# Second MLP: in-projection as seven block products over 768 tokens, weights summed and split ahead and streamed from DRAM

## The chip, the cores and the metric

One core of one Trainium2 chip runs the whole program in one launch. The metric is device time in microseconds (us), the median over runs of the same kernel. The engines are TensorE (PE, with its weight loads listed apart as PEld), VectorE (DVE), ScalarE (ACT), GpSimd (POOL) and SyncE (SP), whose queue issues all DMAs of this kernel. Every engine takes its own instructions in program order and waits for others at semaphores.

## The reference

2304 tokens of width 512 come out of a small chunked attention, and go through two MLPs one after the other, all in float32:

```python
x = attn_out.transpose(0, 2, 1, 3).reshape(2304, 512)   # attention in chunks of 64 tokens
h = x @ w_in1                                           # 512 -> 2048
x = (h * sigmoid(1.702 * h)) @ w_out1                   # 2048 -> 512
h = x @ w_in2                                           # 512 -> 2048
out = (h * tanh(softplus(h))) @ w_out2                  # 2048 -> 512
```

The weights arrive as 64-bit floats and are turned into float32 on the chip.

## The kernel before

**Three products for one.** Each float32 operand is split into a high part (rounded to the fp32r format) and a low part (the rest), and a product is made of three fp32r matmuls, high by high, high by low, low by high. `mm3` issues them (lines 352 to 354). Each matmul has its own load of 128 stationary columns.

**Tiling.** The tokens are cut into 6 blocks of 384 (`NB`, `TB`), the hidden width of 2048 into 16 slices of 128 (`KF`), the model width of 512 into 4 slices (`KD`). The main loop runs n over 6 x 16 slices of the first MLP, then 6 x 16 of the second. One step n is: `in_proj` for block n // 16 and slice n % 16 (12 matmuls of 128x384 into one PSUM bank of the two with tag `h`), the activation on ACT (`gelu`, or `mish` in the second MLP, line 421), its high part (`g_hi`, line 374) and its low part (`g_lo`, line 378), and, two steps late (`LAG`), the out-projection of slice n - 2: `out_a` in the first MLP (12 matmuls of 128x384 into four banks), `out_b` in the second (9 matmuls of 128x512 into three banks, lines 441 to 443, tokens as stationary operand). After the 16th slice `evac_a` (lines 403 and 404) or `evac_b` (449, 451) empties the banks.

**First MLP, beside it.** While the first block runs, the raw weights of the first MLP are loaded, rescaled (`scale`, line 142, ACT), put together from two integer halves (`join`, lines 152 and 153, DVE) and split (line 174 ACT, 185 DVE); all 32 weight tiles then stay in SBUF (pool `wres`, one tag for each). Blocks 2 to 5 have the attention of the next block between their steps: transposes, scores, softmax, product with v, each a step apart, through one PSUM tag `at`. In the same steps the 32 weight tiles of the second MLP are loaded, joined and stored to DRAM as whole float32 (`w_f`, line 157). In the last block, as the first MLP's tiles fall free, they are fetched (`ws`, line 165) and split, on ACT and POOL, into the same 32 places. The second MLP so has all its weights in SBUF.

**Between the MLPs.** `evac_a` writes the first MLP's result as high and low part over the block's own input. The last two blocks stay in SBUF, the others go to DRAM (`xd`) and are loaded again one block ahead (`load_x2`).

**What sets the order.** The order on every engine is that of the program text (`manual_schedule`). All DMAs go through SP's one queue: each entry waits for its own semaphores, and what stands behind it waits too.

Of the kernel before, what the change touches and what calls it, by code (L numbers as in the profile page):

```python
# [35 lines left out]
def tile_kernel(  # L36
# [32 lines left out]
    xp = ctx.enter_context(tc.tile_pool(name="xp", bufs=2))  # L69
# [7 lines left out]
    class Weights:  # L77
# [8 lines left out]
        def __init__(self, w_in, w_out, staged):  # L86
# [7 lines left out]
            self.first, self.ahead = 0, NRAW - 2 if staged else NRAW  # L94
            self.spare = [] if staged else [f"w{kind}{f}" for kind, f in self.order]
            self.at = {"load": 0, "scale": 0, "join": 0, "fetch": 0, "split": 0}
            self.staged = dram.tile([self.np, P, DM], F32, name="w_f32") if staged else None
# [6 lines left out]
        def load(self):  # L104
            if (i := self._next("load")) is None:
                return
            kind, f = self.order[i]
            r = self.room(f"raw{i}")
            if kind == "i":
                src = self.w_in[:, 2 * f * P : 2 * (f + 1) * P]  # L110
                nc.sync.dma_start(
                    out=r.rearrange("p (k f) w -> p k (f w)", k=KD),
                    in_=src.rearrange("(k p) f -> p k f", p=P),
                )
            else:
                nc.sync.dma_start(
                    out=r.rearrange("p f w -> p (f w)"),
                    in_=self.w_out[f * P : (f + 1) * P, :],
                )
            self.raw[i] = r  # L120
# [7 lines left out]
        def load_ahead(self):  # L128

            used = self.at["join"] if self.staged is not None else self.at["split"] - len(self.open)  # L130
# [7 lines left out]
        def scale(self):  # L138
            if (i := self._next("scale")) is None:
                return  # L140
            hi = self.raw[i][:, :, 1].bitcast(F32)
            nc.scalar.activation(hi, hi, AF.Prelu, scale=2.0**-112, alpha=2.0**32)

        def join(self):
            if (i := self._next("join")) is None:
                return
            r = self.raw.pop(i)
            lo, hi = r[:, :, 0], r[:, :, 1]
            to = hi
            if self.staged is not None:  # L150
                to = half_slot(f"wf{i}").bitcast(I32)
            nc.vector.tensor_scalar(lo, lo, 29, None, op0=ALU.logical_shift_right)
            nc.vector.scalar_tensor_tensor(  # L153
                to, hi, 3, lo, op0=ALU.logical_shift_left, op1=ALU.bitwise_or
            )
            if self.staged is not None:
                nc.sync.dma_start(out=self.staged[i], in_=to.bitcast(F32))
            else:
                self.f32[i] = to.bitcast(F32)

        def fetch(self):
            if (i := self._next("fetch")) is None:
                return
            self.f32[i] = half_slot(f"ws{i}")
            nc.sync.dma_start(out=self.f32[i], in_=self.staged[i])

        def split(self):
# [9 lines left out]
            if self.staged is not None:  # L177
                self.rest()

        def rest(self):  # L180

            eng = nc.vector if self.staged is None else nc.gpsimd
            while self.open:
                key, w, hi, lo = self.open.pop(0)
                eng.tensor_tensor(out=lo, in0=w, in1=hi.bitcast(F32), op=ALU.subtract)  # L185
# [7 lines left out]
        def convert(self):  # L193

            if self.at["join"] > self.at["split"] and self.staged is None:
# [6 lines left out]
            if self.staged is not None or self.at["load"] > 4:  # L202
                self.load_ahead()

# [24 lines left out]
    class Attention:  # L229
# [106 lines left out]
        def x_hi(self, copy):  # L336
            j = self.j
            if j not in xh:
                xh[j] = xp.tile([P, KD, TB], F32R, tag="xh", name=f"xh{j}")
                xl[j] = xp.tile([P, KD, TB], F32R, tag="xl", name=f"xl{j}")  # L340
# [54 lines left out]
    xd, x2 = {}, {}  # L395
# [271 lines left out]
```

## Time and profile before

| what | value |
|---|---|
| time, median of 3 runs | 885.21 us (884.06 to 886.15) |
| profiled execution, first to last instruction | 883.0 us |
| PE busy | 867.3 us, 98% of the span |
| DVE, ACT, POOL busy | 353.2, 277.9, 41.4 us |
| matmuls recorded | 5724 |
| moved by DMA | 82.68 MB, mean 94 GB/s |

The page gives no time of the profiled execution other than its span, so sums below are made against 883.0 us, which is 2.2 us under the median. PE is busy nearly throughout. Matmuls overlap in the pipeline: one is listed with some 335 ns, but the next starts 173 ns later, so the cost of one is read from the distance of starts, not from its duration.

### The profile page before, as it was taken

The page shows a single profiled execution, that of the slowest core. Times are in us where ns is not written, and L with a number is a line of the kernel's source. Part 1 is how long each engine was busy: PE and PEld are TensorE (multiplying, and loading weights), DVE is VectorE, ACT ScalarE, POOL GpSimd, SP SyncE. Part 2 cuts the span into 40 slices and gives each one's busy share as a digit, 9 for nine tenths or more (in the row PEclk, how much of TensorE's full clock was granted, in tenths as well). Part 3 has the DMA queues.
Part 4 walks back from the last instruction along what each step waited for, and adds up shares of the span by engine and source line. Part 5 has one row for each costly group of instructions (what it writes and reads, how often), then busy time and mean ns, then how long its engine had stood idle before and what let it go on. Part 6 is the DMA issues. An engine that isn't in the chain of part 4 may idle for free.

```text
span 883.0 us, 13566 instructions
## 1 busy us (share of the span) xinstructions
PE 867.3 (98%) x5724; PEld 810.6 (92%) x5724; DVE 353.2 (40%) x687; ACT 277.9 (31%) x469; POOL 41.4 (5%) x38
## 2 busy tenths in 40 slices
PE   6999999999999999999999999999999999999998
PEld 4799999999999999999999999999999999999997
DVE  6799554554545555554333222222222222222221
ACT  3898543443324434333434111111111111111111
POOL 0000000000000000001664000000000000000000
PEclk9899999999999999999999999999999999999999
DMA  9968633465438256423442001200200200200100
GB/s 238 269 192 253 170 117 99 108 192 131 108 112 210 76 141 179 115 83 129 128 120 61 1 1 36 72 1 26 83 0 15 94 1 2 107 1 0 37 1 36
DMA packets 91934, 82.68 MB, mean 94 GB/s; under 512 B 58848, under 2 KB 75232, under 8 KB 91872
## 3 DMA queue, kind: packets, MB, share of 16 engines
q1 hardware_dynamic: 91872, 81.80, 31.8%
q8 instruction: 45, 0.74, 0.4%
q14 instruction: 17, 0.14, 0.1%
HBM read 62.39 MB, written 19.40 MB: 93 GB/s over the span
## 4 chain that ended last, share of the span: by engine, by line
PE 91%; DVE 6%; ACT 2%; DMA 1%; issue 0%; DVEq 0%; ACTq 0%
PE h L352 15%; PE h L354 14%; PE h L353 14%; PE acc L354 7%; PE acc L353 7%; PE acc L352 7%; PE accb L443 5%; PE accb L442 5%; PE accb L441 5%; PE third L442 3%; PE third L443 3%; PE third L441 2%; DVE raw L153 1%; PE tr L256 1%; PE pv L328 1%; PE sc L273 1%
## 5 line engine op out<-in xcount | busy, mean ns | idle before, releaser
L374 DVE CAST gh<-t 128x384 fp32r<-128x384 f32 x176 | 69.2, 393 | 437.1 <-ACT t L421 295.8
L352 PE MATMUL h<-xh,wi 128*128 128x384 f32 x512 | 177.3, 346 | 0.0
L354 PE MATMUL h<-xh,wi 128*128 128x384 f32 x512 | 171.6, 335 | 1.2 <-DVE wi L185 1.2
L353 PE MATMUL h<-xl,wi 128*128 128x384 f32 x512 | 171.5, 335 | 0.9 <-DVE xl L348 0.9
L421 ACT ACTIVATE t<-h 128x384 f32<-128x384 f32 x96 | 47.2, 492 | 335.2 <-PE h L354 334.4
L353 PE MATMUL acc<-gl,wo 128*128 128x384 f32 x384 | 128.5, 335 | 1.4 <-DVE gl L378 1.4
L354 PE MATMUL acc<-gh,wo 128*128 128x384 f32 x384 | 128.6, 335 | 0.0
L352 PE MATMUL acc<-gh,wo 128*128 128x384 f32 x384 | 128.3, 334 | 0.0
L378 DVE TENSOR_TENSOR gl<-t,gh 128x384 fp32r<-128x384 f32 x192 | 107.2, 558 | 14.8 <-ACT gh L374 2.7
L352 PEld LDWEIGHTS h<-xh,wi 128*128 128x128 f32 x512 | 96.2, 188 | 3.3
L353 PEld LDWEIGHTS h<-xl,wi 128*128 128x128 f32 x512 | 96.3, 188 | 2.4 <-DVE xl L348 1.2
L354 PEld LDWEIGHTS h<-xh,wi 128*128 128x128 f32 x512 | 96.1, 188 | 1.5 <-DVE wi L185 1.5
L354 PE MATMUL h<-x2h,wi 128*128 128x384 f32 x256 | 86.4, 337 | 0.0
L352 PE MATMUL h<-x2h,wi 128*128 128x384 f32 x256 | 86.2, 337 | 0.0
L353 PE MATMUL h<-x2l,wi 128*128 128x384 f32 x256 | 86.0, 336 | 0.0
L370 ACT ACTIVATE t<-h 128x384 f32<-128x384 f32 x96 | 47.1, 490 | 112.4 <-PE h L354 95.5
L443 PE MATMUL accb<-wo,gl 128*128 128x512 f32 x192 | 76.2, 397 | 0.0
L442 PE MATMUL accb<-wo,gh 128*128 128x512 f32 x192 | 75.8, 395 | 0.0
L441 PE MATMUL accb<-wo,gh 128*128 128x512 f32 x192 | 74.6, 389 | 0.0
L353 PEld LDWEIGHTS acc<-gl,wo 128*128 128x128 f32 x384 | 72.1, 188 | 2.0 <-DVE gl L378 2.0
L354 PEld LDWEIGHTS acc<-gh,wo 128*128 128x128 f32 x384 | 72.1, 188 | 0.0
L352 PEld LDWEIGHTS acc<-gh,wo 128*128 128x128 f32 x384 | 72.1, 188 | 0.0
(83 smaller groups left out, 966.5 us busy)
## 6 DMA issues: line engine op xcount, KB each, us to landing
raw<-in_moe_w_in_dram SPq DMA_DIRECT2D x32, 512.0 KB, 4.5
raw<-in_moe_w_out_dram SPq DMA_DIRECT2D x32, 512.0 KB, 4.5
w_f<-wf SPq DMA_DIRECT2D x32, 256.0 KB, 2.2
ws<-w_f SPq DMA_DIRECT2D x32, 256.0 KB, 2.7
out_dram<-o SPq DMA_DIRECT2D x18, 256.0 KB, 2.1
v<-in_v_dram SPq DMA_DIRECT2D x16, 256.0 KB, 5.8
q<-in_q_dram SPq DMA_DIRECT2D x13, 256.0 KB, 4.9
k<-in_k_dram SPq DMA_DIRECT2D x13, 256.0 KB, 5.4
```

What stands on the lines that cost most here:

```text
L153: nc.vector.scalar_tensor_tensor(to, hi, 3, lo, op0=ALU.logical_shift_left, op1=ALU.bitwise_or)
L256: nc.tensor.transpose(self.pt[:, bank, s], src[:, s], ident)
L352: nc.tensor.matmul(o, wh, mh, start=start, stop=False)
L353: nc.tensor.matmul(o, wh, ml, start=False, stop=False)
L354: nc.tensor.matmul(o, wl, mh, start=False, stop=stop)
L370: nc.scalar.activation(gt[n], hp.pop(n), AF.Gelu_apprx_sigmoid)
L374: (nc.scalar.copy if n < KF else nc.vector.tensor_copy)(gh[n], gt[n])
L378: nc.vector.tensor_tensor(out=gl[n], in0=gt.pop(n), in1=gh[n].bitcast(F32), op=ALU.subtract)
L421: nc.scalar.activation(gt[n], h, AF.Mish)
L441: nc.tensor.matmul(o, a[:, ts], wh, start=f == 0, stop=False)
L442: nc.tensor.matmul(o, a[:, ts], wl, start=False, stop=False)
L443: nc.tensor.matmul(o, b[:, ts], wh, start=False, stop=f == KF - 1)
```

## The change

**What it computes differently.** The second MLP's in-projection is taken for pairs of 384-token blocks and pairs of hidden slices (g and g + 8) as a 2 by 2 block product with seven block products in place of eight: the tokens give 2 x 2 blocks (two token blocks by two halves of the model width), the weights 2 x 2 (two halves of the model width by two slices). Sums and differences of weight blocks (t1 to t4) and of token blocks (s1 to s4) are the operands of products p1 to p7; each product has two k-slices, so 6 matmuls of 128x384. The four results are added up in PSUM (p2 onto p1, p3 onto p5, p4 onto p7) and on DVE (`combine`, line 913).

**What moves.** Weights of the second MLP no longer stay in SBUF. `Second.step` loads, rescales and joins them during steps 16 to 82 of the first MLP, forms the sums on DVE, splits everything into high and low part (ACT and DVE, lines 449, 450, 468, 469) and stores it to DRAM: for each of 8 groups 3.5 tiles of 128x1024 for the in-projection (`w_sums`) and 2 for the out-projection (`w_outs`). In the second MLP these are streamed into 21 places in SBUF (`flow_in`, line 750) once for each of the 3 pairs, each place being refilled as its tile is used up. The result of the first MLP goes to DRAM whole (`x2d`). The token operands p1 to p7 of a pair (`Tokens`, and `Staged` for pairs 1 and 2) are computed beside the work of the pair before, stored to DRAM (`x_ops`, line 725) and loaded into nine homes (`load_home`, line 711), the last five during the pair's last group. POOL's subtraction goes.

```diff
-    def mish(n, h):
-        gt[n] = tmp.tile([P, TB], F32, tag="t", name=f"t{n}")
-        nc.scalar.activation(gt[n], h, AF.Mish)
-        g_hi(n)
-        g_lo(n)
...
     def evac_a(j):
-        for m in range(KD // 2):
-            i = acc[j][m][:, :, 0:TB]
-            ho = xh[j][:, 2 * m : 2 * m + 2, :]
-            lo = xl[j][:, 2 * m : 2 * m + 2, :]
-            nc.scalar.copy(ho, i)
-            nc.vector.tensor_tensor(out=lo, in0=i, in1=ho.bitcast(F32), op=ALU.subtract)
...
+        t = xp.tile([P, KD, TB], F32, tag=f"xh{j % 2}", name=f"x2_{j}")
+        for m, copy in enumerate((nc.scalar.copy, nc.vector.tensor_copy)):
+            copy(t[:, 2 * m : 2 * m + 2, :], acc[j][m][:, :, 0:TB])
+        x2[j] = dram.tile([P, KD, TB], F32, name=f"x2d{j}")
+        nc.sync.dma_start(out=x2[j], in_=t)
...
+        def split(self, w, to, name):
+            n = w.shape[-1] // (2 * P)
+            w = w.rearrange("p (u x) -> p u x", u=n)
+            t = wraw.tile([P, n, 2, 2 * P], F32R, tag="raw", name=name)
+            nc.scalar.copy(t[:, :, 0], w)
+            nc.vector.tensor_tensor(
+                out=t[:, :, 1], in0=w, in1=t[:, :, 0].bitcast(F32), op=ALU.subtract
+            )
+            nc.sync.dma_start(out=to, in_=t.bitcast(F32))
...
+        def step(self, s):
...
+            if k == 0:
+                self.scale(b)
+                self.join(a)
+            elif k == 1:
+                self.load(c)
+                self.join(b)
+                self.sum_b(g, "t1")
+            elif k == 2:
+                self.load(d)
+                for t in ("t2", "t3", "t4"):
+                    self.sum_b(g, t)
+                self.split_sums(g, 0)
+            elif k == 3:
+                self.split_sums(g, 1)
+            elif k == 4:
+                self.scale(c)
+                self.split_sums(g, 2)
+                if nxt:
+                    self.load(("i", g + 1))
+            elif k == 5:
+                self.split_sums(g, 3)
+                self.join(c)
+            elif k == 6:
+                self.scale(d)
+                self.split_out(2 * g)
+                if nxt:
+                    self.load(("i", g + 1 + KF // 2))
+            else:
+                self.join(d)
+                if nxt:
+                    self.scale(("i", g + 1))
...
+        def load_home(q):
+            p, i = divmod(q, len(ORDER))
+            both = put_home(p, ORDER[i])
+            for part, t in enumerate(both):
+                nc.sync.dma_start(out=t.bitcast(F32), in_=ops[p][i, :, part])
...
+        def flow_in(tag):
...
+            t = wres.tile([P, 2, DM], F32R, tag=tag, name="f" + "_".join(map(str, key)))
...
+            nc.sync.dma_start(out=t.bitcast(F32), in_=src)
...
+        for n, (p, g) in enumerate(groups):
+            A, Bk = hb[n % 2], hb[(n + 1) % 2]
...
+            if p + 1 < PAIRS and g == 1:
+                tok = Staged(p + 1, work_room, work_room, None)
+                tok.load()
...
+            go("p1", A)
+            nc.scalar.copy(s1, A)
+            before[0]()
+            go("p6", Bk, stop=True)
+            combine(u2, s1, Bk)
+            spare()
+            before[1]()
+            go("p2", A, start=False, stop=True)
+            gone("s", p, g, 0)
+            low11 = activate(A, s1, f"{n}a")
+            go("p5", Bk)
+            gone("s", p, g, 1)
+            combine(c22, u2, Bk)
+            g11 = low11()
+            spare()
+            before[2]()
+            go("p7", A)
+            combine(c22, c22, A)
+            spare()
+            low22 = activate(c22, c22, f"{n}b")
+            go("p3", Bk, start=False, stop=True)
...
+            combine(c12, u2, Bk)
+            g22 = low22()
+            low12 = activate(c12, c12, f"{n}c")
+            spare()
+            before[3]()
+            go("p4", A, start=False, stop=True)
+            gone("s", p, g, 2)
+            combine(c21, u2, A)
+            g12 = low12()
+            g21 = activate(c21, c21, f"{n}d")()
```

`before[0]` to `before[3]` are the four out-projections of the group before (9 matmuls of 128x512 each), `spare` takes one piece of the next pair's token operands, `gone` refills a place of the stream, and `go` also calls `load_home` in a pair's last group.

On PE in the second MLP a whole in-projection of 12 matmuls stood behind each out-projection. Before (h is the in-projection's bank, accb and third those of the out-projection, x2h and x2l the tokens, wi and wo weights, gh and gl the activations):

```order
L441 MATMUL third_5180<-wo10_4962,gh138_6326 128x512
L442 MATMUL third_5180<-wo10_4962,gh138_6326 128x512
L443 MATMUL third_5180<-wo10_4962,gl138_6328 128x512
L352 MATMUL h13_6395<-x2h0_5620,wi13_5008 128x384
L353 MATMUL h13_6395<-x2l0_5621,wi13_5008 128x384
L354 MATMUL h13_6395<-x2h0_5620,wi13_5008 128x384
```

Now (h_0 and h_1 are the two banks of the products, x0p2 the operand of product p2 of pair 0, fs a streamed tile of weight sums, fo of the out-projection, sum_at, sum_acc0 and sum_acc1 the out-projection's banks):

```order
L875 MATMUL sum_acc1_5301<-fo_0_11_5348,gh3b_5636 128x512
L876 MATMUL sum_acc1_5301<-fo_0_11_5348,gh3b_5636 128x512
L877 MATMUL sum_acc1_5301<-fo_0_11_5348,gl3b_5647 128x512
L848 MATMUL h_0_5173<-x0p2__4879,fs_0_4_0_5140 128x384 x6
L848 MATMUL h_1_5174<-x0p5__4802,fs_0_4_1_5227 128x384 x6
L875 MATMUL sum_at_5299<-fo_0_11_5348,gh3c_5650 128x512
L876 MATMUL sum_at_5299<-fo_0_11_5348,gh3c_5650 128x512
L877 MATMUL sum_at_5299<-fo_0_11_5348,gl3c_5675 128x512
```

Products of 6 matmuls stand singly or in twos between out-projections, and a group of four slices has 42 in-projection matmuls where it had 48.

On SP in the second MLP, between two token blocks, before (o are tiles of the result, x2h and x2l the parts of a token block that is loaded ahead):

```order
L453 DMA out_0_dram<-o4_0_5611 128x512
L453 DMA out_0_dram<-o4_1_5614 128x512
L453 DMA out_0_dram<-o4_2_5617 128x512
L415 DMA x2h0_5620<-xd0_1398 128x1536
L416 DMA x2l0_5621<-xd0_1398 128x1536
```

Now, in the last group of pair 0 (x1p2 and so on are homes of pair 1's operands, each loaded in two halves):

```order
L711 DMA x1p2__6055<-x_ops1_606 128x768 x2
L711 DMA x1p5__6074<-x_ops1_606 128x768 x2
L711 DMA x1p7__6093<-x_ops1_606 128x768 x2
L750 DMA fo_1_1_6096<-w_outs_77 128x1024
L711 DMA x1p3__6107<-x_ops1_606 128x768 x2
L750 DMA fo_1_9_6110<-w_outs_77 128x1024
L750 DMA fs_1_3_0_6124<-w_sums_76 128x1024
L711 DMA x1p4_0_6132<-x_ops1_606 128x768
L711 DMA x1p4_1_6133<-x_ops1_606 128x768
```

SP's queue held five entries for a block's 66 us; now it holds weight tiles all through the second MLP, and the next pair's operands among them.

On DVE in the second MLP nothing but `g_hi` and `g_lo` stood between two blocks. Now, in group 1 of pair 1 (u9, v9 and c9 are the group's partial results, gl the low parts of its activations, a11 to a22 the token blocks of pair 2, s3, s2p1 and s2p5 operands made of them):

```order
L913 TENSOR_TENSOR u9_6316<-u9_6316,h_0_5173 128x384
L545 TENSOR_TENSOR s3_2_6350<-a11_2_6319,a21_2_6323 128x768
L913 TENSOR_TENSOR v9_6317<-u9_6316,h_0_5173 128x384
L864 TENSOR_TENSOR gl9a_6384<-u9_6316,gh9a_6373 128x384
L721 TENSOR_TENSOR s2p1_1_6353<-a11_2_6319,s2p1_0_6352 128x768
L913 TENSOR_TENSOR v9_6317<-v9_6317,h_1_5174 128x384
L545 TENSOR_TENSOR a21_2_6323<-a21_2_6323,a22_2_6325 128x768
L913 TENSOR_TENSOR v9_6317<-u9_6316,h_0_5173 128x384
L864 TENSOR_TENSOR gl9b_6423<-v9_6317,gh9b_6412 128x384
```

The subtraction of a21, which has to arrive by DMA first, stands ahead of the additions that empty the product banks.

## Rows read from the trace of the kernel before

**Rows 1.** Busy time by stage: stretch, length, engines' busy us, granted clock, DMA share, GB/s.

```profile
core 0: us, PE busy (x) PEld busy (x) DVE busy (x) ACT busy (x) POOL busy (x), PEclk, DMA share, GB/s
0.00:28.00 28.00, 20.48 (x271) 13.84 (x272) 16.76 (x33) 12.95 (x22) 0.70 (x6) 0.88 0.92 214
28.00:95.00 67.00, 62.49 (x501) 59.25 (x500) 60.43 (x115) 58.73 (x100) 0.00 (x0) 1.00 0.84 251
95.00:410.00 315.00, 315.00 (x2552) 306.14 (x2551) 159.77 (x309) 121.79 (x188) 0.00 (x0) 1.00 0.45 127
410.00:480.00 70.00, 70.00 (x405) 70.00 (x405) 22.87 (x35) 28.75 (x51) 39.43 (x31) 1.00 0.42 121
480.00:879.40 399.40, 399.35 (x2003) 361.38 (x2001) 93.38 (x198) 55.09 (x110) 1.29 (x1) 1.00 0.07 26
879.40:883.00 3.60, 0.00 (x0) 0.00 (x0) 0.00 (x0) 0.57 (x1) 0.00 (x0) 1.00 0.58 219
```

**Rows 2.** Timeline of PE, one step of the second MLP: start us, duration, instruction.

```profile
481.59 0.33 PE L352 MATMUL h<-xh,wi 128*128 128x384 f32 x1
...
483.50 0.33 PE L354 MATMUL h<-xh,wi 128*128 128x384 f32 x1
483.67 0.39 PE L441 MATMUL accb<-wo,gh 128*128 128x512 f32 x1
...
485.75 0.33 PE L352 MATMUL h<-xh,wi 128*128 128x384 f32 x1
```

**Rows 3.** Groups by line and shape: count | busy us, mean ns | idle before.

```profile
L378 DVE TENSOR_TENSOR gl<-t,gh 128x384 fp32r<-128x384 f32 x192 | 107.2, 558 | 14.8 <-ACT gh L374 2.7 <-DVE gh L374 0.5
L421 ACT ACTIVATE t<-h 128x384 f32<-128x384 f32 x96 | 47.2, 492 | 335.2 <-PE h L354 334.4 <-ACT wo L174 0.8
L404 DVE TENSOR_TENSOR xl<-acc,xh 128x768 fp32r<-128x768 f32 x12 | 11.5, 958 | 2.6 <-ACT xh L403 2.1
L185 DVE TENSOR_TENSOR wo<-raw,wo 128x512 fp32r<-128x512 f32 x16 | 11.0, 686 | 1.0 <-ACT wo L174 0.8
L174 ACT CAST wi<-ws 128x512 fp32r<-128x512 f32 x16 | 9.9, 617 | 2.1 <-DMA ws<-w_f 2.1
L403 ACT CAST xh<-acc 128x768 fp32r<-128x768 f32 x12 | 9.6, 802 | 4.5 <-PE acc L354 4.5
L374 ACT CAST gh<-t 128x384 fp32r<-128x384 f32 x16 | 8.2, 514 | 0.4
```

**Rows 4.** DMA issues: count, KB each, median us from issue to landing.

```profile
raw<-in_moe_w_out_dram SPq DMA_DIRECT2D x32, 512.0 KB, 4.5
...
out_dram<-o SPq DMA_DIRECT2D x18, 256.0 KB, 2.1
...
x2h<-xd SPq DMA_DIRECT2D x4, 768.0 KB, 5.0
x2l<-xd SPq DMA_DIRECT2D x4, 768.0 KB, 6.4
```

**Rows 5.** Busy time by stretch while a token block is loaded, columns as in rows 1.

```profile
552.00:554.00 2.00, 2.00 (x12) 1.82 (x11) 0.38 (x1) 0.00 (x0) 0.00 (x0) 1.00 1.04 347
554.00:556.00 2.00, 2.00 (x12) 1.78 (x11) 0.36 (x1) 0.49 (x1) 0.00 (x0) 1.00 0.96 366
```

**Rows 6.** Timeline of PE in those stretches, first and next matmul row of a change of bank.

```profile
552.74 0.33 PE L352 MATMUL h<-xh,wi 128*128 128x384 f32 x1
...
554.84 0.39 PE L441 MATMUL accb<-wo,gh 128*128 128x512 f32 x1
```

**Rows 7.** Timeline of PE at the start, matmuls at both clock levels.

```profile
1.12 5.30 PE L496 MATMUL idle<-zeros 128*128 128x384 bf16 x16 [1.12 <-DVE zeros L476]
...
13.16 2.94 PE L496 MATMUL idle<-zeros 128*128 128x384 bf16 x17
```

More of the change, by code (lines that the diff above doesn't have):

```diff
@@ L93, in __init__ @@
             self.open = []
[L94 to L97, printed above, removed]
+            self.first, self.ahead = 0, NRAW
+            self.spare = [f"w{kind}{f}" for kind, f in self.order]
+            self.at = {"load": 0, "scale": 0, "join": 0, "split": 0}
         def _next(self, what):
@@ L128, in load_ahead @@
         def load_ahead(self):
[L130 removed]
+            used = self.at["split"] - len(self.open)
             while self.at["load"] < self.np and (
@@ L146, in join @@
                 return
[L147 to L165, printed above, removed]
+            self.f32[i] = join_raw(self.raw.pop(i))
         def split(self):
@@ L551, in tile_kernel @@
+        for n in range(4, NA):
             f = n % KF
@@ new lines, in tile_kernel, with bank @@
+            if n > NA - KF + 3 and n - (NA - KF + 4) < 7:
+                tok.part(n - (NA - KF + 4))
+            if n >= NA - KF:
+                gone = 2 * (f + 1) - min(LAG, f + 1)
+                while flow and gone - 6 > 21 - len(flow):
+                    flow_in(flow.pop(0))
+        hb = [ps.tile([P, TB], F32, tag="h", name=f"h_{i}") for i in range(2)]
+        banks = []
+        shared = {}
+        def bank(i):
+            if not banks:
+                for tag in ("at", "acc0", "acc1"):
+                    t = ps.tile([P, 2, 512], F32, tag=tag, name=f"sum_{tag}", bufs=1)
+                    banks.extend((t[:, 0], t[:, 1]))
+            return banks[i]
@@ new lines, in tile_kernel, with evac_b, last_a @@
+        seen = {(p, h): 0 for p in range(PAIRS) for h in range(2)}
+        def evac_b(p, half):
+            for t in range(TT):
+                i = half * TT + t
+                o = wres.tile([P, DM], F32, tag=work[i % len(work)], name=f"o{p}_{i}")
+                (nc.scalar.copy if i % 2 == 0 else nc.vector.tensor_copy)(o, bank(i))
+                r0 = (2 * p * TT + i) * P
+                nc.sync.dma_start(out=out[r0 : r0 + P, :], in_=o)
+        def last_a(m):
+            out_a(m, m // KF, m % KF)
+            if m == NA - 1:
+                evac_a(m // KF)
@@ new lines, in tile_kernel, with gone, work_room, combine @@
+        before = [lambda: last_a(NA - 2), lambda: last_a(NA - 1), lambda: None, lambda: None]
+        side = []
+        assert not flow
+        def gone(*key):
+            flow_in(place.pop(key))
+        def work_room(name):
+            shared["n"] = shared.get("n", -1) + 1
+            return wres.tile([P, 2, TB], F32, tag=work[shared["n"] % len(work)], name=name)
+        add, sub = ALU.add, ALU.subtract
+        def combine(out, x, h, op=add):
+            nc.vector.tensor_tensor(out=out, in0=x, in1=h, op=op)
@@ L639 @@
+        for i in (0, 2, 1, 3):
+            before[i]()
 _INS = ["q", "k", "v", "moe_w_in", "moe_w_out", "moe2_w_in", "moe2_w_out"]
```

402 lines of the change are left out of this document (290 added, 112 removed).

## The prediction

> **What bounds the kernel now.** I read the busy time by stage first [rows 1]. From 95 us to the last matmul at 879.4 us PE is busy all the time (315.00 of 315.00, 70.00 of 70.00, 399.35 of 399.40 us), at a granted clock of 1.00, the upper of the two levels. In the second MLP DVE works 93.4 and ACT 55.1 of 399.4 us, and the DMA engines are busy for 0.07 of it. So there the time is the number of PE's instructions by their distance, and nothing else ends last. Before 95 us DVE and ACT (60.4 and 58.7 of 67 us) and the loads bound the kernel; the change leaves that part as it is. Next I read the distance of PE's starts in one step of the second MLP [rows 2]: 12 in-projection matmuls take 481.59 to 483.67, 2.08 us or 0.173 us each, and 9 out-projection matmuls 483.67 to 485.75, 2.08 us or 0.231 us each. A matmul's listed duration of 0.33 us covers two neighbours at once and prices nothing. A change of bank is free: from the last in-projection matmul (483.50) to the next bank's first (483.67) are 0.17 us.
>
> **The change, part by part.**
>
> *In-projection of the second MLP.* Removed: 96 steps by 12, 1152 matmuls of 128x384. Added: 24 groups by 7 products by 6, 1008 of the same shape. The difference is 144 by 0.1733 = 25.0 us. All of it lies on PE, which has no idle time there [rows 1], so all of it can be had. The out-projection keeps 24 by 36 = 864 matmuls, and the first MLP its own. A group becomes 42 by 0.1733 + 36 by 0.231 = 7.3 + 8.3 = 15.6 us, the second MLP 24 by 15.6 = 374 us.
>
> *New waits inside a group.* Products use two banks by turns, and each needs DVE or ACT to have read its bank. In a steady group one out-projection (2.08 us) and one product (1.04 us) lie between, 3.1 us of cover. Behind it stand, at most, one addition of 128x384 on DVE (nearest row 0.56 us) or one Mish on ACT (0.49 us) [rows 3]. In order of DVE's queue: five additions and four low parts by 0.56 are 5.0 us a group; beside them in groups 1 to 4 of pairs 0 and 1 some two pieces of token operands, four operations of 128x768 by 0.96, 3.8 us; in all 8.8 of 15.6. ACT has four Mish, four high parts by 0.51 and a copy, 4.5 us, and two casts of 0.80. The narrowest place is the last addition (c21), which stands behind two low parts and a side piece: I find it done 1.7 us before PE wants its bank. The very first group has no out-projections for its last five products, so a cover of 1.04 us against 0.5 to 0.6 us of work and the hand-over. Bounds: 0 and 1 us a pair, 3 in all; I take 0.5, since all but one place have cover of two or more times the work.
>
> *The stream.* A group eats 5.5 tiles of 0.524 MB, 2.88 MB in 15.6 us, 185 GB/s. 21 tiles are asked for ahead of the second MLP; the other 111 (58 MB), the operands of pairs 1 and 2 (3.1 MB read, 11.0 stored, 11.0 loaded), 4.7 MB of results and 0.8 MB of the first MLP's last block make 89 MB in 374 us, 238 GB/s. While a token block was loaded in the kernel before, with PE at full pace, 347 and 366 GB/s went at a share near 1 [rows 5], and the matmuls kept 12 in 2.10 us [rows 6]. So I expect a share of 0.65 to 0.7, and PE unharmed. A tile is asked for some four groups (60 us) before use, against 4.5 us to land [rows 4]. The narrow part is the operands. In a pair's last group 2.88 + 5 by 0.786 = 6.8 MB are asked for in 15.6 us, 436 GB/s: at 350 that ends 3.9 us late. Each home is filled behind the product that frees it and wanted one group later, 18.7 us on; less some 9 us (queue and landing) a margin of 10 us stays. In group 1 DVE waits for the third of four token loads: about 7 us into the group, in pair 1 about 8 us, since the place it lands in holds a result until that is stored; its addition is wanted by PE at 11.4 us. Cost 0 in the forecast. The lower bound of the rate is that of the stages with small pieces, 251 GB/s at a share of 0.84 or 127 at 0.45 [rows 1], both over 280 at full share; then the last group's queue is 9 us, still inside the margin.
>
> What the rows show of many pieces at once is that the two loads of 768 KB, asked for half a microsecond apart, land in 5.0 and 6.4 us [rows 4], so they share the time. The Trainium skill, DMA: Bandwidth & Descriptors (section Bandwidth, Measured), speaks against this change: it asks to batch transfers to 1 MiB and more, and gives 6.15 us for 1 MB alone. By half of that a tile takes an estimated 3.1 us and a group 17 us of transfer, if no two overlap, so the second MLP would be bound by the stream; the trace does not agree, since pieces overlap.
>
> *First MLP.* DVE gains 32 sums of 128x256 (I take 0.43 us, carried down from 0.56 and 0.69 [rows 3]), 40 subtractions of 128x512 by 0.69 and 8 of half that, and the first pair's operands: 14 + 27 + 3 + 10 = 54 us, less 6 of the lighter evacuation. It goes from about half of 315 us to 0.65. ACT gains 40 casts by 0.62 and 8 of half that, 27 us, and loses the 32 casts it did after 410 us. POOL's 39 us go, which nobody waited for. Loads stay, and stores grow from 8.4 to 23 MB. What hides all this is the step of some 4.2 us: what DVE and ACT make in one is used by PE one step later (attention) or two (activations), and PE has not idled with DVE at half load. SP's queue is new at one point: stores wait for DVE, a load waits for the store whose place it takes, and the attention tiles' loads stand behind; those are fetched five steps (over 20 us) ahead. If the cover goes, a transpose or score waits a microsecond or two at some of the 15 attention tiles. Bounds 0 and 8 us; I take 0.5, the nearer row being PE's 315.00 of 315.00.
>
> *The end.* From the last matmul 3.6 us remain [rows 1]: copy, store, landing, as before.
>
> **Sum.** 883.0 - 25.0 + 0.5 + 0.5 = 859.0 us of span; with the 2.2 us by which the median stands above it, **861 us**. PE alone gives 860.2.
>
> **The rivals.**
>
> *Late operands and a busier first MLP.* The 25.0 us are had, but waits at the two pair switches (3 us each if the mixed traffic goes at 235 GB/s in place of 350) and at some attention tiles (up to 8 us) return 3 to 13: 864 to 873, middle 867. For it: SP's queue is in order, and DVE's share grows by a third. Against: margins of 10 us and of a step.
>
> *Hand-offs.* A group has 11 changes between products and out-projections, with two banks that ACT and DVE must clear; before, there were two in 4.2 us with a whole step of cover. If each of 168 products paid 0.1 us, 17 us would go: 878; at 0.15 us nothing is left, 885. Against: changes of bank cost nothing [rows 2, 6]. In the first microseconds, where the granted clock averages 0.88 [rows 1], a matmul of 384 columns took 0.33 us, and 0.173 later [rows 7]: the levels of 1.2 and 2.4 GHz. A tenth of the second MLP at the lower one would cost 37 us and end at 898. The Trainium skill, TensorE: Matmul & The Clock Gate (A second HAM failure mode), tells of a kernel whose clock oscillated because PE idled briefly as it cycled through PSUM banks; the rows here show a clock of 1.00 over 192 such changes.
>
> *The stream bounds the second MLP (slower).* The place is `flow_in` with `x_ops` on one queue. 89 MB in 374 + 25 us is the point from which it decides: below 223 GB/s sustained the kernel is slower than before. At 200 the second MLP takes 445 us and the program 932; at 214, the rate of the first 28 us [rows 1], 416 and 903. For it: the mean demand of 238 lies above that row, reads and writes are mixed, and nothing before ran so for long. Against: that row holds many small attention loads at a share of 0.92, and rows 5 show 347 and more. If pieces did not overlap at all, a group would take 5.5 by the 4.5 us of one tile [rows 4], 24.8 us, 9.2 too many in some 20 groups, and the program 1045; by rows 4 this has hardly a chance, 0.01 of this case.
>
> **How the numbers follow.** Forecast with small waits, 858.5 to 864: 0.74. Late operands or first MLP, 864 to 873: 0.12. Hand-offs with most of the gain lost, 873 to 883.4: 0.05. Within 0.2%, about what a measurement of this kernel can tell from no change: 0.02. Slower, stream or clock: 0.06. Below 858.5: 0.01, as no other PE work goes. The range of 8 in 10 is 858.5 to 869; it leaves out the end of the second case and the rarer ones. Faster 0.92, same 0.02, slower 0.06.
>
> **What would show it.** Right: 5580 matmuls recorded; PE busy all of the second MLP in about 374 us; groups 15.6 us apart; a DMA share near 0.7 there; no PE wait of over a microsecond on an operand or a tile. Wrong: PE waiting for a DMA at the first groups of pairs 1 and 2 or at `fs` and `fo` tiles (stream), for DVE's additions inside groups (hand-offs), for attention tiles after 95 us (first MLP), a granted clock under 1.00, or a distance of matmuls above 0.173 and 0.231 us while the DMAs run.

## The result and the profile after

The changed kernel takes **862.88 us** (median of 4 runs, 861.68 to 863.58) beside 884.97 us of the kernel before on the same chip: a ratio of 0.975, with a 95% interval of 0.9736 to 0.9764. The forecast was 861.0, with a range of 858.5 to 869.0. The profiled execution took 861.68 us, of which 859.9 are its span.

The busy time by stage, to be laid beside [rows 1] (same columns; the second MLP's first product starts at 471.95 us):

```profile
28.00:95.00 67.00, 63.33 (x505) 60.34 (x506) 61.05 (x116) 59.94 (x103) 0.00 (x0) 1.00 0.83 250
95.00:410.00 315.00, 315.00 (x2551) 306.16 (x2550) 192.82 (x380) 141.84 (x229) 0.00 (x0) 1.00 0.53 160
410.00:480.00 70.00, 70.00 (x406) 70.00 (x405) 27.74 (x48) 17.20 (x29) 0.00 (x0) 1.00 0.63 207
480.00:856.00 376.00, 373.53 (x1851) 335.23 (x1849) 138.71 (x245) 122.15 (x237) 0.00 (x0) 1.00 0.68 235
```

The first MLP is read first. DVE went from 159.77 to 192.82 of 315 us and ACT from 121.79 to 141.84, and PE still has 315.00 of 315.00. In the second MLP the DMA engines went from a share of 0.07 to 0.68 at 235 GB/s, with the clock at 1.00 and PE working all but 2.5 of 376 us (0.6 of those lie behind the last matmul). PE's waits from 95 us to the end are three (what waited, for what; us in all, times, longest):

```profile
PE h L848 <- DVE v L913: 0.9, 1, 0.9
PE sum_acc L875 <- ACT o L890: 0.7, 1, 0.7
PE h L848 <- ACT u L858: 0.4, 1, 0.4
```

None is for a tile of the stream. One product and one out-projection of a steady group, to be laid beside [rows 2] (timeline of PE: start, duration, instruction):

```profile
514.75 1.20 PE L848 MATMUL h<-x0p__4763,fs 128*128 128x384 f32 x6
515.79 0.39 PE L875 MATMUL sum_at<-fo,gh2a 128*128 128x512 f32 x1
...
517.64 0.39 PE L877 MATMUL sum_acc<-fo,gl2a 128*128 128x512 f32 x1
517.87 1.23 PE L848 MATMUL h<-x0p__4841,fs 128*128 128x384 f32 x6
518.94 0.39 PE L875 MATMUL sum_acc<-fo,gh2b 128*128 128x512 f32 x1
```

The six matmuls of a product take 1.04 us (514.75 to 515.79), or 1.07 where an out-projection of 512 columns stands ahead of it (517.87 to 518.94), and the nine of an out-projection 2.08 us (515.79 to 517.87), as before. Groups are counted from 0 through all three pairs, and an out-projection is named by the group whose activations it uses; it runs one group later. The starts of one out-projection from group to group lie 15.68 us apart in pairs 0 and 1 and 15.73 in pair 2, up to the last group, with one exception: from group 8 to group 9 it is 17.42 us.

Four stages can now be put beside each other. "Start" ends where the transposes of the attention behind the first token block begin (`at<-ident,e`), the second MLP goes from its first matmul's start to its last one's, and the end is the rest of the span. All are us of the profiled execution; the span is given to 0.1 us, so the ends and their difference are good to about that:

| kernel | start | first MLP | second MLP | end | span |
|---|---|---|---|---|---|
| before | 94.87 | 378.40 | 405.69 | 4.04 | 883.0 |
| after | 93.55 | 378.40 | 383.08 | 4.87 | 859.9 |
| difference | -1.32 | 0.00 | -22.61 | +0.83 | -23.1 |

The -1.32 are no gain of the change: among ten executions of the changed kernel and its variants the start ends between 93.55 and 96.35 us, and this one is the shortest. So the change removed about 21.8 us, where the forecast has 25.0 for the 144 matmuls alone. The experiments ask where the rest went, and whether the covers on which the forecast rested are as thick as it said.

### The profile page after: what moved, and what is told of

Same layout as the page of the kernel before. It is cut to its first block, busy times and chain, and to the rows that moved or that the text cites. A ratio compares the mean times of both kernels' runs of the same rounds, so it can differ in the third digit from the quotient of the medians.

```text
span 859.9 us, 13861 instructions
## 1 busy us (share of the span) xinstructions
PE 841.3 (98%) x5580; PEld 784.9 (91%) x5580; DVE 438.5 (51%) x821; ACT 354.5 (41%) x617; POOL 0.7 (0%) x6
## 4 chain that ended last, share of the span: by engine, by line
PE 87%; DVE 5%; DMA 3%; ACT 3%; issue 0%; SPq 0%; DVEq 0%; ACTq 0%
PE h L848 20%; PE h L342 7%; PE acc L344 7%; PE acc L343 7%; PE acc L342 7%; PE h L343 7%; PE h L344 7%; PE sum_acc L876 5%; PE sum_acc L877 5%; PE sum_acc L875 5%; PE sum_at L877 2%; PE sum_at L876 2%; PE sum_at L875 2%; PE tr L246 1%; DVE raw L190 1%; DMA out_dram<-o 1%
## 5 line engine op out<-in xcount | busy, mean ns | idle before, releaser
L342 PE MATMUL h<-xh,wi 128*128 128x384 f32 x384 | 134.2, 350 | 0.0
L344 PE MATMUL h<-xh,wi 128*128 128x384 f32 x384 | 128.4, 334 | 1.3 <-DVE wi L152 1.3
L343 PE MATMUL h<-xl,wi 128*128 128x384 f32 x384 | 128.5, 335 | 0.9 <-DVE xl L338 0.9
L360 ACT ACTIVATE t<-h 128x384 f32<-128x384 f32 x96 | 47.1, 491 | 129.0 <-PE h L344 119.5
L364 DVE CAST gh<-t 128x384 fp32r<-128x384 f32 x80 | 28.8, 360 | 100.1 <-ACT t L360 100.1
L342 PEld LDWEIGHTS h<-xh,wi 128*128 128x128 f32 x384 | 72.1, 188 | 2.0
L344 PEld LDWEIGHTS h<-xh,wi 128*128 128x128 f32 x384 | 72.1, 188 | 1.6 <-DVE wi L152 1.6
L343 PEld LDWEIGHTS h<-xl,wi 128*128 128x128 f32 x384 | 72.2, 188 | 1.1 <-DVE xl L338 1.1
L913 DVE TENSOR_TENSOR v<-u,h 128x384 f32<-128x384 f32 x48 | 26.6, 553 | 83.8 <-PE h L848 83.8
L368 DVE TENSOR_TENSOR gl<-t,gh 128x384 fp32r<-128x384 f32 x96 | 53.5, 557 | 5.4 <-ACT gh L364 2.7
L858 ACT ACTIVATE v<-v 128x384 f32<-128x384 f32 x48 | 25.2, 525 | 65.6 <-DVE v L913 65.6
L913 DVE TENSOR_TENSOR u<-u,h 128x384 f32<-128x384 f32 x24 | 13.3, 554 | 46.2 <-PE h L848 46.2
L913 DVE TENSOR_TENSOR v<-v,h 128x384 f32<-128x384 f32 x24 | 13.3, 554 | 36.3 <-PE h L848 36.3
L913 DVE TENSOR_TENSOR c<-u,h 128x384 f32<-128x384 f32 x24 | 13.2, 552 | 31.0 <-PE h L848 31.0
```

Source lines behind the costliest of these rows:

```text
L342: nc.tensor.matmul(o, wh, mh, start=start, stop=False)
L343: nc.tensor.matmul(o, wh, ml, start=False, stop=False)
L344: nc.tensor.matmul(o, wl, mh, start=False, stop=stop)
L360: nc.scalar.activation(gt[n], hp.pop(n), AF.Gelu_apprx_sigmoid)
L364: (nc.scalar.copy if n < KF else nc.vector.tensor_copy)(gh[n], gt[n])
L368: nc.vector.tensor_tensor(out=gl[n], in0=gt.pop(n), in1=gh[n].bitcast(F32), op=ALU.subtract)
```

## Experiments

**The kernel again, with two places mended apart and together.** `after_again` is the changed kernel once more. The others stand on it.

> The changed kernel once more, for its time beside the runs that follow: 861.5 to 863.6 us, as in its four runs. In its trace the second MLP from its first in-projection matmul to its last matmul is some 383 us long, the first MLP after 95 us as long as before.

It took 864.48 us (ratio 0.977, 0.9755 to 0.9785), span 862.8. The stages are 96.11, 378.39, 383.44 and 4.86: of the 2.9 us of span by which it differs from the first execution 2.6 are in the start and 0.4 in the second MLP.

`e1_banks` gives the two halves of the out-projection's six banks another order, so that a copy and a matmul at the very end don't meet in one tile of two banks. Its second edit gives ACT the first and third copy of the second half, in place of DVE; the copies of the first half, for one of which PE waited, stay on the engines that they had:

```
-            return banks[i]
+            return banks[(0, 1, 2, 4, 5, 3)[i]]
...
-                (nc.scalar.copy if i % 2 == 0 else nc.vector.tensor_copy)(o, bank(i))
+                (nc.scalar.copy if t % 2 == 0 else nc.vector.tensor_copy)(o, bank(i))
```

> The out-projection's six banks are dealt out differently: the third result tile of both halves shares a PSUM tile, the first two of the second half have one of their own, and ACT takes the first and third copy. Theory: in the changed kernel PE waited 0.7 us for a copy out of the other bank of the same PSUM tile at the end, and the last two copies came one after the other behind the last matmul, 0.8 us more than before; both go, so 1.6 us less than the changed kernel, 861.3, with no PE wait for a copy in the last 10 us and 4.0 us from the last matmul's start to the end. Rival: the end is set by the stores' landing and the wait merely moves, so no change beyond 0.3 us.

`e2_side_later` loads the next pair's token blocks in group 1 as before, but starts the work on them a group later:

```
             if p + 1 < PAIRS and g == 1:
                 tok = Staged(p + 1, work_room, work_room, None)
                 tok.load()
+            if p + 1 < PAIRS and g == 2:
                 for i in range(len(ORDER)):
```

> The token loads of the next pair stay where they are, at the start of group 1, but the work on them begins one group later. Theory: PE's two waits in group 1 of the second pair (0.4 and 0.9 us, with their restarts 1.6 us) come from DVE and ACT standing in front of a token load that waits for a result's store; they go, so 861.3, 1.6 us under the changed kernel. Rival: the late stores hold up something else in that place (the stream or the staging of operands), and the time stays within 0.4 us, or operands now come too late at the pair switch and it rises.

Times and the second MLP of these (the exception is the time from group 8 to group 9 over the 15.68 us of the others):

| kernel | us, ratio (interval) | second MLP | exception | second MLP less exception |
|---|---|---|---|---|
| after | 862.88, 0.975 (0.9736 to 0.9764) | 383.08 | 1.74 | 381.34 |
| after_again | 864.48, 0.977 (0.9755 to 0.9785) | 383.44 | 2.09 | 381.35 |
| e1_banks | 863.31, 0.9758 (0.9745 to 0.9771) | 382.31 | 1.95 | 380.36 |
| e2_side_later | 861.80, 0.9733 (0.972 to 0.9747) | 381.34 | 0.00 | 381.34 |

The medians alone would not carry this, since their intervals overlap; the stages do, to 0.01 us. Moving the side work by a group takes away the exception and nothing else; the other order of banks takes away 0.98 us and nothing else (`e1_banks` keeps an end of 4.87 us). In the list of waits `e2_side_later` keeps one wait of PE from 95 us on, that of the end, and `e1_banks` those two of group 9:

```profile
PE sum_acc L875 <- ACT o L890: 0.7, 1, 0.7
```

```profile
PE h L848 <- DVE v L913: 1.0, 1, 1.0
PE h L848 <- ACT u L858: 0.4, 1, 0.4
```

What happens in group 9 is read from the timelines of the kernel after, here in order of time by engine: DVE, SP, ACT, DVE again, and PE (the bracket names what ended an idle stretch and how long that was):

```profile
610.09 0.69 DVE L890 COPY o<-sum_acc 128x512 f32<-128x512 f32 x1 [2.38 <-DMA out_dram<-o]
...
608.38 3.06 SPq L892 DMA_DIRECT2D out_dram<-o  x3
...
615.40 1.75 SPq L541 DMA_DIRECT2D a<-x2d  x4
...
618.53 0.83 ACT L718 CAST s2p<-a 128x768 fp32r<-128x768 f32 x1 [5.80 <-DMA a<-x2d]
...
620.50 0.96 DVE L545 TENSOR_TENSOR s<-a,a 128x768 f32<-128x768 f32 x1 [6.66 <-DMA a<-x2d]
...
619.81 1.32 PE L848 MATMUL h<-x1p__6093,fs 128*128 128x384 f32 x6 [0.36 <-ACT u L858]
621.98 1.33 PE L848 MATMUL h<-x1p__6107,fs 128*128 128x384 f32 x6 [0.85 <-DVE v L913]
```

It is a chain of landings. The token blocks land in places that have just held the first pair's result. There are five such places for a pair's six result tiles, so DVE's last copy waits 2.38 us for an earlier result tile to be stored; its own store has to land too, and SP issues the four token loads only at 615.40. SP's list of waits has one line for that:

```profile
SPq L541 <- DMA out_dram<-o: 3.4, 1, 3.4
```

The group's first product had started at 608.8 us. So the loads are asked for 6.6 us into the group, the subtraction that waits for the third of them starts at 11.7 us, and both queues stand behind the loads: ACT's with a Mish behind the cast of the first one, DVE's with the addition that empties a bank behind that subtraction.

`e5_both` has both mends:

> Both the other bank order and the token work one group later. Theory: the two places are far apart and on PE's path both, so the gains add up: 3.2 us under the changed kernel, 859.7. Rival: one of them only; 861.3.

It took 860.61 us (0.9723, 0.9709 to 0.9738), span 858.2, with stages of 94.52, 378.40, 380.37 and 4.91 us. The list of PE's waits from 95 us on is empty, and every group but the first and the last is 15.68 to 15.73 us long. So 405.69 - 380.37 = 25.32 us is what the change takes off a second MLP without waits, 0.1758 us for each of the 144 matmuls.

**One product twice.** If PE sets the time of a group, a further product must cost its own 1.04 us in each of 24 groups; if the hand-offs or the stream do, less.

```
             go("p4", A, start=False, stop=True)
+            product(p, g, "p4", A, False, True)
```

> Product p4 is computed twice onto the same bank (the four results of each group are wrong by that much), 24 times 6 matmuls more, as many as the change took away. Theory (PE sets the second MLP's time): 144 times 0.1755 us, 25.3 us more than the changed kernel, 888, and the DMA share falls by the same part. Rival (the stream or the hand-offs already set part of the time): the added matmuls fall partly into waits, so clearly less, 865 to 883.

It took 887.11 us (1.0032, 1.0019 to 1.0046), 22.6 more than `after_again`. Groups are 16.72 us apart, 1.04 more each. The second MLP is 407.00 us: less the bank's 0.98 and an exception that shrank to 0.54, that is 405.48, or 380.36 and 24 times 1.047. So 144 matmuls added cost 25.1 us, nearly the 25.3 that 144 taken away gave: the group had no slack. That the exception shrank by somewhat more than the product's own length fits a wait behind a longer group.

**More traffic on the same queue.** `e4_half` and `e4_full` ask for tiles that nobody uses, one behind each refill of an out-projection tile or behind every refill. Four of the stream's 21 places are given up for them, so tiles are also asked for later.

```
-        flow, work = freed[6:27], freed[27:]
+        flow, waste, work = freed[6:23], freed[23:27], freed[27:]
...
+            if banks and key[0] == "o":
+                i = shared["x"] = shared.get("x", -1) + 1
+                w = wres.tile([P, 2, DM], F32, tag=waste[i % 4], name=f"waste{i}")
+                nc.sync.dma_start(out=w, in_=second.outs[i % KF])
...
-                while flow and gone - 6 > 21 - len(flow):
+                while flow and gone - 6 > 17 - len(flow):
```

In `e4_full` the condition is `if banks and True:`, and in both two lines that set `banks` and `shared` stand further up. The lines below stand three further down in both (L851 is L848 of the kernel after, L893 L890 and L916 L913).

> More traffic: 17 places for the stream in place of 21, and behind every out-projection tile that is streamed in the second MLP another tile of 0.52 MB is loaded into one of four places and not used: 44 tiles, 23 MB. The stretch then asks for some 114 MB in 376 us, 303 GB/s, at a share near 0.87. Theory (PE sets the time, the stream has room up to about 345 GB/s): within 1 us of the changed kernel but for up to 4 us at the two pair switches, 862 to 867. Rival (the room is small, since reads and writes are mixed): the second MLP stretches by 10 us or more.

> As the last, but an unused tile behind every tile of the stream: 115 tiles, 60 MB, 151 MB in all. Theory: the stream now sets the time; at the 346 GB/s that the changed kernel's 235 GB/s at a share of 0.68 come to, the second MLP takes 436 us, so about 920, with the share near 1 and PE waiting for stream tiles and operands. If the limit lies nearer 400 GB/s (two slices before showed 442), 865 to 880; if mixed traffic is held to 300, 980.

`e4_half` took 867.9 us (0.9804, 0.979 to 0.9819) and `e4_full` 907.44 (1.0249, 1.0233 to 1.0264). Their second MLPs, from 472 us to the end, in the columns of [rows 1]:

```profile
472.00:866.10 394.10, 385.95 (x1908) 347.29 (x1906) 141.97 (x250) 125.63 (x242) 0.00 (x0) 0.99 0.79 288
```

```profile
472.00:903.70 431.70, 392.46 (x1902) 350.47 (x1901) 141.39 (x249) 125.64 (x241) 0.00 (x0) 0.96 0.89 348
```

At 288 GB/s all that is lost lies in the exception, which grows from 1.74 to 6.30 us: 387.64 - 6.30 is 381.34 again. So a quarter more traffic than the change asks for cost the stream nothing, and one chain of landings 4.2 to 4.6 us. At 348 GB/s the loss has places too. Here are five stretches of `e4_full`, of which the second and the fourth hold the pair switches, and the first three of eight lines on what PE waited for from 95 us on:

```profile
472.00:590.00 118.00, 118.00 (x598) 107.69 (x598) 46.14 (x79) 40.17 (x75) 0.00 (x0) 1.00 0.93 367
590.00:650.00 60.00, 42.17 (x179) 35.91 (x178) 14.99 (x26) 13.16 (x26) 0.00 (x0) 0.83 1.01 394
650.00:715.00 65.00, 65.00 (x325) 58.67 (x324) 28.05 (x48) 24.38 (x47) 0.00 (x0) 1.00 1.03 412
715.00:790.00 75.00, 58.75 (x273) 51.70 (x273) 17.92 (x34) 16.25 (x32) 0.00 (x0) 0.91 1.01 399
790.00:903.70 113.70, 108.54 (x534) 96.51 (x532) 34.28 (x63) 31.68 (x63) 0.00 (x0) 1.00 0.61 232
```

```profile
PE h L851 <- DVE c L916: 22.2, 2, 11.6
PE h L851 <- DMA x2p__7325<-x_ops: 3.4, 2, 3.0
PE h L851 <- DMA x1p<-x_ops: 3.2, 2, 3.0
...
```

Even with the DMA engines at a share of 1.03 and 412 GB/s PE works 65.00 of 65 us, and it never waits for a tile of weights. It waits at the switches: mostly for DVE (24 us in three waits), which waits for a result to be stored and then for a token load, and less for the new pair's operands (10 us).

```profile
631.54 0.69 DVE L893 COPY o<-sum_acc 128x512 f32<-128x512 f32 x1 [20.23 <-DMA out_dram<-o]
...
644.13 0.96 DVE L545 TENSOR_TENSOR s<-a,a 128x768 f32<-128x768 f32 x1 [8.44 <-DMA a<-x2d]
```

So the rival "the stream bounds the second MLP" decides from another point than its mean rate: what gives first, in `e4_half` and here, is a result's store among the stream's tiles, on the same queue.

**Products back to back.** `e6_back_to_back` takes the four out-projections out from between the products and does them behind the group's last product, which leaves one product (1.04 us) as the cover of a hand-off:

```
-            before[0]()
...
-            before[1]()
...
-            before[2]()
...
-            before[3]()
...
             combine(c21, u2, A)
+            for b in before:
+                b()
```

> The seven products of a group stand one behind the other, and the four out-projections of the group before follow in one piece, so that every product has 1.05 us of cover for its bank in place of 3.1. Theory: ACT or DVE need 0.6 to 0.8 us from a product's end, so groups without token work lose at most 0.3 us, and the 8 groups with it, where an operation of 0.96 us stands ahead of the addition, 1 to 3 us: 866 to 888, PE waiting for additions on DVE. Rival (hand-offs cost nothing with or without the out-projections between): 862 to 864.

It took 886.49 us (1.0012, 0.9999 to 1.0025): in this order the whole gain is gone. Yet it is not lost in the steady groups. Groups 5, 6, 7, 13, 14, 15 and 18 to 22 take 15.51 to 15.54 us from first product to first product, 0.16 less than in the kernel after. So 1.04 us cover an addition or a Mish, and the six changes saved between 384 and 512 columns cost PE at most 0.027 us each; as the kernel before has eight of these in four slices too, they cancel. What is lost lies in the groups with side work and beside them. Over 15.52 us it is 7.9 in group 1, 11.6 in group 9, 1.4 each in groups 2, 10 and 17, 1.0 each in 8 and 16, and some 0.65 each in 3, 4, 11 and 12; group 0 takes 0.8 more than in the kernel after. In group 1, where no result has to be stored first and the kernel after loses nothing, PE waits 3.45 us behind the cast of a token block, and in group 9 5.58 us behind the same chain as above (ACT, then PE, for either group):

```profile
492.88 0.83 ACT L718 CAST s1p__5308<-a 128x768 fp32r<-128x768 f32 x1 [4.78 <-DMA a<-x2d]
...
494.15 1.60 PE L848 MATMUL h<-x0p,fs 128*128 128x384 f32 x6 [3.45 <-ACT u L858]
```

```profile
632.28 0.83 ACT L718 CAST s2p<-a 128x768 fp32r<-128x768 f32 x1 [7.95 <-DMA a<-x2d]
...
633.56 2.29 PE L848 MATMUL h<-x1p__6075,fs 128*128 128x384 f32 x6 [5.58 <-ACT u L858]
```

The side work stands in the program behind single products. With these close together DVE comes to the first subtraction of group 1 2.9 us into the group, 2.1 us sooner than in the kernel after, and waits 6.68 us there for the landing, in place of 3.39. How much of the loss in groups 1 and 9 is this, how much the lower clock behind the waits (granted 0.86 from 486.38 to 498.50 us, and 0.81 from 622.20 to 649.30), and how much the wait of ACT's casts for the out-projections behind the products was not taken apart. So what this run shows is that the products' places between the out-projections cover the side work; a steady group does not need them.

**The end.** `e5_both` had no wait left and still 4.91 us behind the last matmul's start, where the kernel before has 4.04. `e7_tail` stands on it and does the last two out-projections of the second half tile by tile, six matmuls a tile in place of three and three:

```
-        for i in (0, 2, 1, 3):
-            before[i]()
+        before[0]()
+        before[2]()
+        p, last = PAIRS - 1, ((KF - 1, g22), (HALF - 1, g21))
+        for t in range(TT):
+            ts = slice(t * P, (t + 1) * P)
+            for j, (f, gs) in enumerate(last):
+                w = item["o", p, f]
+                nc.tensor.matmul(bank(TT + t), gs[0][:, ts], w[:, 0], start=False, stop=False)
+                nc.tensor.matmul(bank(TT + t), gs[0][:, ts], w[:, 1], start=False, stop=False)
+                nc.tensor.matmul(bank(TT + t), gs[1][:, ts], w[:, 0], start=False, stop=j == 1)
+        evac_b(p, 1)
```

> The version with both mends, and at the very end the last two out-projections of the second half done token tile by token tile (six matmuls a tile, as the kernel before had them) in place of one whole out-projection after the other (three a tile). Theory: the 0.8 us more behind the last matmul come from the order of the ends, since with three matmuls a tile the second tile is finished only 0.7 us ahead of the end and all three stores pile up behind it; with six, copies and stores of the first two tiles lie beside PE's work: tail 4.1 to 4.3 us in place of 4.9, a median near 859.9. Rival: the tail is the transfer of stores beside late traffic or fixed latency: tail 4.9 as before the edit, median 860.6. The second MLP's PE time stays 380.4 us.

It took 859.4 us (0.9719, 0.9705 to 0.9732), with stages of 94.56, 378.40, 380.36 and 4.28. The copies of the second half in `e7_tail` (ACT, DVE, ACT), those of `e5_both`, and the first one of the kernel before:

```profile
852.39 0.59 ACT L890 COPY o<-sum_acc 128x512 f32<-128x512 f32 x1 [2.13 <-PE sum_acc L993]
...
853.01 0.69 DVE L890 COPY o<-sum_acc 128x512 f32<-128x512 f32 x1 [2.71 <-ACT o L890]
...
853.79 0.59 ACT L890 COPY o<-sum_acc 128x512 f32<-128x512 f32 x1 [0.81 <-PE sum_acc L993]
```

```profile
853.03 1.31 ACT L890 COPY o<-sum_acc 128x512 f32<-128x512 f32 x2 [2.81 <-PE sum_acc L877]
...
853.65 0.69 DVE L890 COPY o<-sum_acc 128x512 f32<-128x512 f32 x1 [3.39 <-ACT o L890]
```

```profile
878.03 0.59 ACT L449 COPY o<-accb 128x512 f32<-128x512 f32 x1 [4.26 <-PE accb L443]
```

With six matmuls a tile the first copy starts 0.93 us ahead of the last matmul (853.32), as in the kernel before (878.96), in place of 0.26 ahead (853.29), and some 0.6 of the 0.9 us come back. The median's step from `e5_both` is within the intervals; the stage is not. This version beats both kernels.

## Why the prediction was right, and by what it missed

The likeliest case came, with the sign, inside the case's own range, 1.9 us above the forecast. Term by term, in us of span:

| term | forecast | measured | by |
|---|---|---|---|
| 144 matmuls less | -25.0 | -25.32 | e5_both against before |
| hand-offs in groups | +0.5 | 0.00 | all steady groups of one length |
| stream | 0 | 0.00 | no wait on `fs` or `fo`; e4_half |
| first MLP | +0.5 | 0.00 | 378.40 in each |
| token loads, group 1 of pair 1 | 0 | +1.74 (2.09 again) | e2_side_later |
| end: one tile of two banks | 0 | +0.98 | e1_banks |
| end: copies and stores | 0 | +0.83 | e7_tail gives some 0.6 back |
| start | 0 | -1.32 | varies from run to run |

The sum of the measured column is -23.1, that of the two spans. Between span and median lie 3.0 us in place of the 2.2 that I added, as the execution profiled was the shortest of four. That the span of 859.9 came within 0.9 us of the forecast 859.0 is in part luck: 3.55 us were lost in three places at which nothing was put, and 2.6 of them were met by two allowances of 0.5 that were not needed, by 0.3 more from the matmuls and by the 1.3 of a short start.

**The matmul term.** All of it could be had, because PE had no idle time to absorb it [rows 1], and `e3_p4_twice` and `e5_both` show that this held after the change as well. The distance taken from one step [rows 2], 0.1733 us, is 0.1758 over the whole. "A change of bank is free" had been read in one direction only: in the step of [rows 2] the in-projection still stands behind an out-projection of the first MLP, of 384 columns. In the steady step of [rows 6], behind one of 512 columns, twelve take 2.10 us (552.74 to 554.84) in place of 2.08, and six in the kernel after 1.07 in place of 1.04. With four such places a group is 15.68 us long and not 15.6; the kernel before has four in four steps as well, so little of it is left in the difference.

**Hand-offs.** The thought that nearly all places have cover of twice the work was right, and too careful with its 0.5: `e6_back_to_back` shows that a steady group without side work bears a third of that cover. The rival's 0.1 us for each of 168 products would have been 17 us; nothing of it is seen. The Trainium skill, TensorE: Matmul & The Clock Gate (A second HAM failure mode), tells of a kernel whose clock oscillated because PE idled briefly between groups of matmuls as it cycled through PSUM banks. Here PE cycles through the banks without idling, and the second MLP keeps 1.00 over 24 groups of 11 products and out-projections each.

**The stream.** The forecast had 238 GB/s at a share of 0.65 to 0.7, and it is 235 at 0.68. What [rows 5] said of two microseconds holds for 65 at 412 GB/s, so the point of 223 GB/s was passed with much to spare. A piece of the stream can take longer to land than [rows 4] say, without harm, as it is asked for four groups ahead. The second MLP's issues (count, KB each, median us to landing), in the kernel after and then in `e4_full`:

```profile
fs<-w_sums SPq DMA_DIRECT2D x69, 512.0 KB, 5.1
...
out_dram<-o SPq DMA_DIRECT2D x18, 256.0 KB, 5.1
```

```profile
fs<-w_sums SPq DMA_DIRECT2D x71, 512.0 KB, 9.3
...
out_dram<-o SPq DMA_DIRECT2D x18, 256.0 KB, 6.9
```

The Trainium skill, DMA: Bandwidth & Descriptors (section Bandwidth, Measured), asks to batch transfers to 1 MiB and more. Pieces of half that would have bound the second MLP if they did not overlap: 5.5 tiles of a group at 5.1 us each would be 28 us. The trace shows that they do, with groups of 15.68 us, and that the engines were not at their limit with them, at a share of 0.68.

**The first MLP.** DVE's share is 0.61, where I had put 0.65. That PE's 315.00 of 315.00 would stay was the nearer of my two bounds, and is what came; at what DVE load the 8 us of the other would come no run here shows.

**The step that was mis-sized** is the third of four token loads in group 1 of pair 1, for which DVE was to wait until about 8 us into the group, wanted at 11.4, at a cost of 0. The mechanism and the place were right, and the time was 11.7 us. In pair 0, where the loads wait for no result, the same subtraction started 8.4 us into group 1 (491.79, the group's first product at 483.39; forecast about 7) and PE did not wait. So the wait for a result's store was priced at some 1 us and took 3.3. The only landing of a result tile that the prediction had is that of a quiet queue, 2.1 us [rows 4]; in the kernel after it is 5.1, for the same 256 KB, and the two stores of this chain took 5.8 (604.21 to 610.00) and 4.5 (610.81 to 615.33). The 3.4 us of margin could not take that, and the change itself makes the traffic that stretches the chain: the loss of 1.7 us at 235 GB/s is 6.3 at 288. That ACT, too, waits for a token load, with a Mish behind it, was not in the prediction; PE's first wait, of 0.36 us, was for that.

**The step that was left out** is the end. "Copy, store, landing, as before" read the 3.6 us of [rows 1] as a constant, and did not ask which matmul finishes which tile: with three matmuls a tile the three tiles are done within 1.4 us and their copies and stores pile up behind the last. The wait ahead of it, for ACT's copy out of one bank while the matmul goes into the other of the same tile, can be seen in the order of the banks alone, ahead of any run:

```profile
851.04 0.50 PE L875 MATMUL sum_acc<-fo,gh23b 128*128 128x512 f32 x1 [0.68 <-ACT o L890]
```

Whether the chip or only the program's bookkeeping by tiles asks for that wait was not tried. Also open is what remains of the end, 0.1 to 0.3 us.

## What to carry to other kernels

Here PE had no idle time, so the saving of matmuls came back in full. What was lost again was found by subtracting stages and group lengths rather than medians: the two losses inside the second MLP, 1.74 and 0.98 us, were each removed alone, and removed together they give their sum to 0.01 us. When a change fills a queue that was empty, price each chain that passes through it (store, free place, load) with landings under that traffic, not with those of the trace of before. Put work that waits for a load a group later than the load, and look at the last tiles by the order in which they finish, not by the time that the end took before.

## What was not expected of the hardware

The DMA engines went at 412 GB/s over 65 us while PE lost nothing, and what rose was the landing: a piece of 512 KB (`fs`) took 9.3 us in the median of that second MLP, 5.1 in that of the kernel after at 230 to 235 GB/s, and 4.5 in the kernel before [rows 4].

In the second MLP the clock fell where PE waited some microseconds, and was 1.00 in the stretches without such waits. In the stretch of `e4_full` with waits of up to 10.59 us the granted clock was 0.83, and six matmuls behind the longest of these took 2.29 us, as the six of `e6_back_to_back` above behind 5.58 us, where six behind a wait of 0.36 us took 1.32 in the kernel after:

```profile
632.75 2.29 PE L851 MATMUL h<-x1p__5977,fs 128*128 128x384 f32 x6 [10.59 <-DVE c L916]
```

These are the two levels of [rows 7], 1.2 and 2.4 GHz. So part of what a long wait costs is paid behind it; how much of `e4_full`'s 43 us was that was not measured apart.
